# Attention and two expert layers on one core: a second buffer for the split sums, and ScalarE copies in place of four VectorE transposes a group

## The chip, the cores and the metric
One NeuronCore of a Trainium2 chip runs the whole kernel. The metric is the device time of one execution in microseconds. A core has TensorE (PE in the profile; PEld is its weight load), VectorE (DVE), ScalarE (ACT), GpSimd (POOL) and SyncE (SP, which here issues nearly all DMA transfers). Each engine works through its own queue in order.

## The reference
```python
def _attn_ref(q, k, v, beta):                  # 4 x 8 heads, 768 tokens, 48 wide
    k_n = k / (norm(k) + 1e-06)
    for t in range(S):
        y[:, :, t] = einsum('bhd,bhde->bhe', q[:, :, t], state)
        v_old = einsum('bhde,bhd->bhe', state, kt)
        state = state + bt * einsum('bhd,bhe->bhde', kt, vt - v_old)

def _moe_ref(x, w_gate, w1, w2):               # 3072 x 384, 8 experts of 1024
    P = exp(logits - max); 8 rounds of row and column scaling of P
    out = sum over e of P[:, e:e+1] * (maximum(x @ w1[e], 0) @ w2[e])

def _moe2_ref(x, w_in, w_out):                 # 384 -> 2048 -> 384
    h = x @ w_in
    return (h / (1 + exp(-1.702 * h))) @ w_out
```
The three run one after the other, all in float32.

## The kernel before, in words
**Attention stage** (about the first 560 us). The recurrence is done in 24 units of 64 tokens. For each group of four units a generator `prep` (L208) makes 32 inverse triangles of 64x64 in blocks of 32x32: `gram` multiplies keys, and VectorE writes the masked result into `am` (L187); VectorE transposes blocks of `am` into `ln` (L265 and L268), runs the triangle's 30 steps (L271 to L279), and transposes back into `ta` (L297) and `tt` (L324); `pz` and `px` (L302, L311) are the small products between the blocks, whose results ScalarE copies. `chain` (L336) uses `tt` to carry the state. The list at L326 is the order in which `pz`, `px` and the transposes of `tt` are emitted; each `yield` is a place where other work is put in between. Expert 0's matmuls are spread between these pieces, and what is emitted first stands first in each engine's queue. In the first group `gram` also lets ScalarE copy its second plane (L198).

**Expert stages** (about 561 us to the end). A product of a 3x3 scheme of blocks is computed with 15 products instead of 18: `SCHEME` lists them, one a step. Every step emits one product (3 matmuls, L478 to L480, with the results taken by ScalarE L1005, VectorE L1012), the second layer's matmuls of the unit before, and then single calls of generators that prepare later work. 72 units of 15 steps follow each other: 56 for the experts (ReLU, L969 on ScalarE and L971 on VectorE) and 16 for the last layer (sigmoid, L975, L977, L978, L980).

**The sums.** The scheme needs sums of token blocks (`sums`, L543). For each of four chunks of 128 columns, three transfers load `raw` from DRAM (L565, braw in the profile), GpSimd forms sums in `v` (L549, bv), and `put` (L551) splits two or three of them into a rounded part and a rest and writes them to DRAM. `put` is this:
```python
o = bp.tile([128, 2, 3, 128], F32R, tag="o", name="bo")     # one buffer
nc.scalar.copy(out=o[:, 0, 0:n], in_=src)
yield
tt(o[:, 1, 0:n], src, o[:, 0, 0:n].bitcast(F32), ALU.subtract)
yield
for k in range(n):
    nc.sync.dma_start(out=xs[i][hf][at + k, ...], in_=o[:, :, k])
```
After its last line `put` returns, and the same call of the generator goes on to the next sums and the next `put`, up to that one's first `yield`. The generator is called once per slot in the attention stage (L748), and by L1106 at every fifth step, at three steps of five, or at every step of a unit but the first, for the second to the fourth of the four runs of `sums`. `weights1d` (L859) does the like for weights; its tile wo (L869) took the tags raw and o by turns.

Of the kernel before, what the change touches and what calls it, by code (L numbers as in the profile page):

```python
# [10 lines left out]
F32R = mybir.dt.float32r  # L11
# [29 lines left out]
class Attention:  # L41
# [166 lines left out]
    def prep(self, g):  # L208

        nc, am, tt = self.nc, self.am, self.tt  # L210
# [51 lines left out]
                yield 1.0  # L262

        ln = self.one.tile([128, 32, 32], F32, tag="ln", name="ln")
        nc.vector.transpose(out=ln, in_=am[:, :, 32:64].rearrange("p m t -> p t m"))  # L265
        yield 1.0
        for q in (0, 64):
            nc.vector.transpose(out=ln[q:q + 32], in_=am[q:q + 32, :, 0:32].rearrange("p m t -> p t m"))  # L268
            yield 1.0
        nc.vector.memset(ln.rearrange("p t s -> p (t s)")[:, 0:1024:33], 1.0)  # L270
        for jj in range(1, 31):  # L271
            tmp = self.one.tile([128, 256], F32, tag="lt", name="lt")
# [3 lines left out]
                out=t3, in0=ln[:, jj + 1:32, jj:jj + 1].to_broadcast([128, nr, jj]),  # L276
# [42 lines left out]
                nc.scalar.copy(out=tt[q:q + 32, m0:m0 + n, 32:64], in_=ps[q:q + 32])  # L319

        def tr(q):
            p = slice(0, 128) if q is None else slice(q, q + 32)
            c = 32 if q is None else 0
            nc.vector.transpose(out=tt[p, :, c:c + 32].rearrange("p m t -> p t m"), in_=ln[p])  # L324

        for f, *i in (((pz, 0, 16), (tr, None), (pz, 16, 16), (tr, 0), (px, 0, 16), (tr, 64), (px, 16, 16)) if g else  # L326
                      ((pz, 0, 8), (tr, None), (px, 0, 8), (tr, 0), (tr, 64), (pz, 8, 8), (px, 8, 8),
                       (pz, 16, 16), (px, 16, 16))):
            while f == tr and self.upped < u - 1:
                yield 1.0  # L330
            f(*i)
            if (f, i) == (tr, [64]):
                self.ready = g
            yield 1.0

# [104 lines left out]
def kernel(  # L440
# [4 lines left out]
    nc = tc.nc  # L445
# [27 lines left out]
    def split(dst_hi, dst_lo, src, eng=nc.vector):  # L473
        nc.scalar.copy(out=dst_hi, in_=src)  # L474
        eng.tensor_tensor(out=dst_lo, in0=src, in1=dst_hi.bitcast(F32), op=ALU.subtract)  # L475
# [8 lines left out]
    bp = ctx.enter_context(tc.tile_pool(name="b", bufs=1, side="right"))  # L484
# [58 lines left out]
    def sums(i, hf):  # L543


        g = nc.gpsimd

        def tt(o, a, b, op):
            g.tensor_tensor(out=o, in0=a, in1=b, op=op)  # L549

        def put(at, src):  # L551

            n = src.shape[1]
            o = bp.tile([128, 2, 3, 128], F32R, tag="o", name="bo")
            nc.scalar.copy(out=o[:, 0, 0:n], in_=src)
            yield
            tt(o[:, 1, 0:n], src, o[:, 0, 0:n].bitcast(F32), ALU.subtract)
            yield
            for k in range(n):
                nc.sync.dma_start(out=xs[i][hf][at + k, :, :, c:c + 128].bitcast(F32), in_=o[:, :, k].bitcast(F32))  # L560

        for c in range(0, 512, 128):
            raw = bp.tile([128, 3, 3, 128], F32, tag="raw", name="braw")
            for t in range(3):
                nc.sync.dma_start(out=raw[:, t], in_=xf[i][hf][t, :, :, c:c + 128])  # L565
            b = [[raw[:, t, d] for t in range(3)] for d in range(3)]
            v = bp.tile([128, 8, 128], F32, tag="v", name="bv")
            yield
            if i:
                yield from put(8, raw[:, 0:3, 0])  # L570
            tt(v[:, 4], b[2][1], b[2][2], ALU.subtract)
            tt(v[:, 5], b[0][0], b[1][0], ALU.add)
            tt(v[:, 0], b[1][2], v[:, 4], ALU.add)
            tt(v[:, 1], v[:, 4], b[0][2], ALU.subtract)
            yield
            if i:
                yield from put(11, raw[:, 1:3, 1])
            tt(v[:, 2], v[:, 5], b[1][1], ALU.subtract)
            tt(v[:, 3], v[:, 2], v[:, 1], ALU.subtract)
            tt(v[:, 3], v[:, 3], b[0][1], ALU.subtract)  # L580
            yield from put(0, v[:, 0:2])
            tt(v[:, 4], b[1][2], v[:, 5], ALU.subtract)
            tt(v[:, 5], b[1][1], b[1][0], ALU.subtract)
            tt(v[:, 5], v[:, 5], b[2][0], ALU.add)
            yield from put(2, v[:, 2:4])
            tt(v[:, 6], b[0][2], b[2][0], ALU.subtract)
            tt(v[:, 6], v[:, 6], b[2][2], ALU.add)
            tt(v[:, 7], zero, b[1][2], ALU.subtract)
            tt(v[:, 7], v[:, 7], b[2][0], ALU.subtract)
            yield from put(4, v[:, 4:6])  # L590
            if i:
                yield from put(13, raw[:, 0:2, 2])
            yield from put(6, v[:, 6:8])
            yield
# [102 lines left out]

    prep = chain.from_iterable(A.prep(g) for g in range(NG))
    next(prep)
    ew = weights0()  # L700
    A.at[14] = A.at[26] = lambda: next(ew)
    while A.ready < 0:
        next(prep)
# [11 lines left out]
    def slot(t):  # L715

        n, k = rate * ITEMS[t % 16] if t >= LAG else 0, (PIECES if t > 15 else FIRST)[t % 16]
        if t == LAG:
            expert(BURST)
        i = 0  # L720
        while i < k:
            expert(n / (k + 1) * step[0])
            step[0] = next(prep, 1.0)
            i += step[0]
        expert(n / (k + 1))
# [78 lines left out]
    def raw1(e, k):  # L804
        t = xp.tile([128, 2, 3, 128], F32, tag="w1r", name="w1r")
        nc.sync.dma_start(out=t.rearrange("p a b c -> p (a b c)"),
                          in_=w_src(e, k)[0].rearrange("p a b c -> p (a b c)"))
        return t
# [15 lines left out]
    def add1(f):  # L824

        g = nc.gpsimd
        v = xp.tile([128, 12, 128], F32, tag="w1v", name="w1v")
        two = [128, 2, 128]
        g.tensor_tensor(out=v[:, 0:3], in0=f[:, 0], in1=f[:, 1], op=ALU.add)
        yield  # L830
        g.tensor_tensor(out=v[:, 3:5], in0=f[:, 0, 0:1].to_broadcast(two), in1=f[:, 0, 1:3], op=ALU.subtract)
        yield
        g.tensor_tensor(out=v[:, 5:7], in0=f[:, 1, 0:1].to_broadcast(two), in1=f[:, 1, 1:3], op=ALU.subtract)
        yield
        g.tensor_tensor(out=v[:, 7:9], in0=f[:, 0, 1:3], in1=f[:, 1, 0:1].to_broadcast(two), op=ALU.add)
        yield
        g.tensor_tensor(out=v[:, 9], in0=v[:, 5], in1=f[:, 1, 2], op=ALU.subtract)
        yield
        g.tensor_tensor(out=v[:, 10], in0=f[:, 0, 2], in1=v[:, 9], op=ALU.subtract)
        g.tensor_tensor(out=v[:, 11], in0=v[:, 9], in1=f[:, 0, 1], op=ALU.subtract)  # L840
        yield
        yield (12, 14, f[:, 0, 1:3]), (14, 15, f[:, 1, 0:1]), (0, 6, v[:, 0:6]), (6, 12, v[:, 6:12])
# [16 lines left out]
    def weights1d(n):  # L859

        f = raw1(*second[n])
        yield
        for parts in add1(f):
            if parts is None:
                yield
        for a, b, src in parts:
            for c in range(a, b, 2):
                m = min(2, b - c)
                o = bp.tile([128, 2, 2, 128], F32R, tag=("raw", "o")[c // 2 % 2], name="wo")  # L869
                split(o[:, 0, 0:m], o[:, 1, 0:m], src[:, c - a:c - a + m], nc.gpsimd)  # L870
                yield
                nc.sync.dma_start(out=wd[nf + n][:, :, c:c + m].bitcast(F32), in_=o[:, :, 0:m].bitcast(F32))
# [192 lines left out]
    for j in range(len(units) + 1):  # L1065
# [3 lines left out]
        for k in range(len(SCHEME)):  # L1069
            now = 15 * j + k  # L1070
            if (j, k) == (nf + 1, 5):
                building.append(sums(1, 0))
                building.extend(weights1d(n) for n in range(ns))
            elif (j, k) == (2 * nf + 1, 5):
                building.append(sums(1, 1))
# [91 lines left out]
```

## Time and profile before

| | |
|---|---|
| median of 3 runs | 2385.11 us (2384.11 to 2388.26) |
| the profiled execution | 2387.82 us |
| its span, first to last instruction | 2386.1 us |
| mean granted TensorE clock | 0.957 |
| busy share: PE, DVE, ACT, POOL | 92%, 66%, 43%, 47% |
| mean DMA rate | 141 GB/s |

The profile is one execution. Busy shares are means over stages that have different limits, so the rows below are taken by stretch. A wait is the idle time of an engine just before an instruction, with the instruction or transfer that released it. The span is 1.7 us shorter than that execution's own time.

### The profile page before, as it was taken

What the parts mean: (1) busy time and instruction counts of PE and PEld (TensorE: products, weight loads), DVE (VectorE), ACT (ScalarE), POOL (GpSimd) and SP (SyncE); (2) the same over time, 40 slices, a digit from 0 to 9 for tenths busy, and PEclk for the clock granted to TensorE, in tenths of its full rate; (3) what the DMA queues carried; (4) which work ended last, traced back from release to release, by engine and by line L of the source; (5) the groups of instructions that cost most, each with busy time, mean ns of one, the idle gap of its engine ahead of it and who ended that gap; (6) DMA issues with size and microseconds to landing.
All of it is one profiled execution on the core that took longest, in us unless ns stands there. A gap on an engine that the chain in (4) does not pass through costs nothing. (4 is left out here: it accounts for less than half of the span.)

```text
span 2386.1 us, 40806 instructions
## 1 busy us (share of the span) xinstructions
PE 2190.5 (92%) x15663; PEld 1966.7 (82%) x15663; DVE 1565.8 (66%) x2778; ACT 1034.5 (43%) x2101; POOL 1124.5 (47%) x1326
## 2 busy tenths in 40 slices
PE   4599989988889898999999989999999998779999
PEld 3488878887779798999998878898989987668888
DVE  8778786627566575777666566777765555457675
ACT  2233333434334443444445434454544454345554
POOL 5511123225666665666643555566554325543233
PEclk8599999999999999999999999999999998889999
DMA  5223333346343343233367555555554284446331
GB/s 121 55 75 88 98 108 81 101 131 249 116 168 112 116 163 121 102 141 134 118 235 222 156 154 176 176 187 187 183 182 149 87 277 129 117 133 212 119 117 50
DMA packets 229155, 336.75 MB, mean 141 GB/s; under 512 B 15648, under 2 KB 192416, under 8 KB 224800
## 3 DMA queue, kind: packets, MB, share of 16 engines
q1 hardware_dynamic: 228240, 333.26, 43.4%
q8 instruction: 123, 2.02, 0.4%
q10 hardware_dynamic: 720, 0.89, 0.1%
q14 instruction: 72, 0.59, 0.1%
HBM read 204.58 MB, written 129.50 MB: 140 GB/s over the span
## 5 line engine op out<-in xcount | busy, mean ns | idle before, releaser
L479 PE MATMUL po<-w2c,h 128*128 128x384 f32 x1728 | 592.8, 343 | 0.0
L480 PE MATMUL po<-w2c,h 128*128 128x384 f32 x1728 | 590.9, 342 | 0.7 <-DVE h L980 0.7
L478 PE MATMUL po<-w2c,h 128*128 128x384 f32 x1728 | 585.5, 339 | 0.7 <-ACT ye L1034 0.5
L478 PE MATMUL c<-xt,w1c 128*128 128x512 f32 x1080 | 438.9, 406 | 94.2 <-DVE h L971 46.6
L1035 POOL TENSOR_TENSOR acc<-acc,ye 128x384 f32<-128x384 f32 x252 | 264.3, 1049 | 440.6 <-ACT ye L1034 426.9
L480 PE MATMUL c<-xt,w1c 128*128 128x512 f32 x1080 | 434.1, 402 | 0.0
L479 PE MATMUL c<-xt,w1c 128*128 128x512 f32 x1080 | 433.7, 402 | 0.0
L1012 DVE TENSOR_TENSOR o<-o,c 128x512 f32<-128x512 f32 x288 | 197.3, 685 | 271.1 <-PE c L480 231.0
L478 PEld LDWEIGHTS po<-w2c,h 128*128 128x128 f32 x1728 | 330.3, 191 | 41.5 <-ACT ye L1034 1.1
L479 PEld LDWEIGHTS po<-w2c,h 128*128 128x128 f32 x1728 | 328.9, 190 | 40.7
L1037 DVE SCALAR_TENSOR_TENSOR acc<-po,P,acc 128x384 f32<-128x384 f32 x420 | 258.3, 615 | 151.5 <-PE po L480 148.2
L480 PEld LDWEIGHTS po<-w2c,h 128*128 128x128 f32 x1728 | 329.5, 191 | 1.1 <-DVE h L980 1.1
L478 PEld LDWEIGHTS c<-xt,w1c 128*128 128x128 f32 x1080 | 206.2, 191 | 130.5 <-DVE h L971 61.1
L1034 ACT ACTIVATE ye<-po,P 128x384 f32<-128x384 f32 x252 | 146.3, 581 | 300.1 <-PE po L480 290.6
L480 PEld LDWEIGHTS c<-xt,w1c 128*128 128x128 f32 x1080 | 206.1, 191 | 46.3 <-POOL w1c L475 0.4
L479 PEld LDWEIGHTS c<-xt,w1c 128*128 128x128 f32 x1080 | 207.0, 192 | 8.8
L1005 ACT COPY o<-c 128x512 f32<-128x512 f32 x288 | 163.5, 590 | 58.7 <-PE c L480 57.9
L1047 POOL TENSOR_TENSOR acc<-acc,ye 128x384 f32<-128x384 f32 x84 | 92.6, 1102 | 193.3 <-ACT ye L1046 189.9
L969 ACT ACTIVATE h<-c 128x512 fp32r<-128x512 f32 x168 | 96.1, 597 | 164.5 <-DVE c L1012 158.6
L475 POOL TENSOR_TENSOR w2c<-w2r,w2c 128x384 fp32r<-128x384 f32 x140 | 144.6, 1033 | 44.4 <-ACT w2c L474 44.3
L1012 DVE TENSOR_TENSOR f<-o,c 128x512 f32<-128x512 f32 x216 | 149.2, 691 | 12.5 <-PE c L480 3.7
L971 DVE SCALAR_TENSOR_TENSOR h<-f,h 128x512 fp32r<-128x512 f32 x168 | 115.0, 685 | 48.3 <-ACT h L969 47.9
(174 smaller groups left out, 3551.3 us busy)
## 6 DMA issues: line engine op xcount, KB each, us to landing
w1c<-wd SPq DMA_DIRECT2D x210, 384.0 KB, 4.4
wd<-w1c SPq DMA_DIRECT2D x28, 1920.0 KB, 6.9
xs<-bo SPq DMA_DIRECT2D x184, 128.0 KB, 2.2
xt<-xs SPq DMA_DIRECT2D x46, 512.0 KB, 6.0
w2r<-in_w_dram SPq DMA_DIRECT2D x55, 384.0 KB, 6.1
wd<-wo SPq DMA_DIRECT2D x56, 256.0 KB, 2.9
w1r<-in_w_dram SPq DMA_DIRECT2D x28, 384.0 KB, 7.6
x<-in_kq_dram SPq DMA_DIRECT2D x24, 384.0 KB, 6.4
```

Of the source, the lines that this page charges most:

```text
L475: eng.tensor_tensor(out=dst_lo, in0=src, in1=dst_hi.bitcast(F32), op=ALU.subtract)
L478: nc.tensor.matmul(ps, lhs[0], rhs[0], start=start, stop=False, **kw)
L479: nc.tensor.matmul(ps, lhs[0], rhs[1], start=False, stop=False, **kw)
L480: nc.tensor.matmul(ps, lhs[1], rhs[0], start=False, stop=stop, **kw)
L969: nc.scalar.activation(out=h[:, 0], in_=src, func=ACTF.Relu)
L971: nc.vector.scalar_tensor_tensor(out=h[:, 1], in0=src, scalar=0.0, in1=h[:, 0].bitcast(F32), op0=ALU.max, op1=ALU.subtract)
L1005: nc.scalar.copy(out=o, in_=ps)
L1012: nc.vector.tensor_tensor(out=d, in0=o, in1=ps, op=ALU.add if how == "add" else ALU.subtract)
L1034: nc.scalar.mul(ye, ps, P[:, u, e:e + 1])
L1035: nc.gpsimd.tensor_tensor(out=a, in0=a, in1=ye, op=ALU.add)
L1037: nc.vector.scalar_tensor_tensor(out=a, in0=ps, scalar=P[:, u, e:e + 1], in1=a, op0=ALU.mult, op1=ALU.add)
L1047: nc.gpsimd.tensor_tensor(out=a, in0=a, in1=ye, op=ALU.add)
```

## The change
The tile o gets two buffers, in `put` and in `weights1d` (where both tags become o). In `prep`, two ScalarE copies bring two quadrants of `am` into the columns 0 to 31, after which one transpose of all 128 partitions reads those columns, in place of one transpose of all partitions and two of 32. For `tt`, one transpose of all partitions stays and two ScalarE copies take the place of two transposes of 32; in the list of pieces they now stand ahead of the first `px`.
```diff
         ln = self.one.tile([128, 32, 32], F32, tag="ln", name="ln")
-        nc.vector.transpose(out=ln, in_=am[:, :, 32:64].rearrange("p m t -> p t m"))
+
+        for q in (32, 96):
+            nc.scalar.copy(out=am[q:q + 32, :, 0:32], in_=am[q:q + 32, :, 32:64])
+            yield 1.0
+        nc.vector.transpose(out=ln, in_=am[:, :, 0:32].rearrange("p m t -> p t m"))
         yield 1.0
-        for q in (0, 64):
-            nc.vector.transpose(out=ln[q:q + 32], in_=am[q:q + 32, :, 0:32].rearrange("p m t -> p t m"))
-            yield 1.0
...
         def tr(q):
-            p = slice(0, 128) if q is None else slice(q, q + 32)
-            c = 32 if q is None else 0
-            nc.vector.transpose(out=tt[p, :, c:c + 32].rearrange("p m t -> p t m"), in_=ln[p])
-
-        for f, *i in (((pz, 0, 16), (tr, None), (pz, 16, 16), (tr, 0), (px, 0, 16), (tr, 64), (px, 16, 16)) if g else
-                      ((pz, 0, 8), (tr, None), (px, 0, 8), (tr, 0), (tr, 64), (pz, 8, 8), (px, 8, 8),
+            if q is None:
+                nc.vector.transpose(out=tt[:, :, 32:64].rearrange("p m t -> p t m"), in_=ln)
+            else:
+                nc.scalar.copy(out=tt[q:q + 32, :, 0:32], in_=tt[q:q + 32, :, 32:64])
+
+        for f, *i in (((pz, 0, 16), (tr, None), (pz, 16, 16), (tr, 0), (tr, 64), (px, 0, 16), (px, 16, 16)) if g else
+                      ((pz, 0, 8), (tr, None), (tr, 0), (tr, 64), (px, 0, 8), (pz, 8, 8), (px, 8, 8),
                        (pz, 16, 16), (px, 16, 16))):
...
-            if (f, i) == (tr, [64]):
+            if f == px and i[0] == 0:
                 self.ready = g
...
-            o = bp.tile([128, 2, 3, 128], F32R, tag="o", name="bo")
+            o = bp.tile([128, 2, 3, 128], F32R, tag="o", name="bo", bufs=2)
...
-                o = bp.tile([128, 2, 2, 128], F32R, tag=("raw", "o")[c // 2 % 2], name="wo")
+                o = bp.tile([128, 2, 2, 128], F32R, tag="o", name="wo", bufs=2)
```
The second buffer moves no instruction. The copies do. ScalarE's queue at the start of the first group, before (x_125 and x_126 are the operands of `gram`, pg its result):
```order
L128 ACTIVATE ns<-ss 128x16 x2
L198 COPY x_125<-pg 64x512 x4
L198 COPY x_126<-pg 64x512 x4
L128 ACTIVATE ns<-ss 128x16 x2
L198 COPY x_127<-pg 64x512 x4
```
And now:
```order
L128 ACTIVATE ns<-ss 128x16 x2
L198 COPY x_125<-pg 64x512 x4
L198 COPY x_126<-pg 64x512 x4
L267 COPY am<-am 32x32x32 x2
L128 ACTIVATE ns<-ss 128x16 x2
L198 COPY x_127<-pg 64x512 x4
```
The two copies of `am` stand behind the first eight copies of `gram`'s second plane.

ScalarE's queue at the end of the first group, before:
```order
L474 CAST w2s_198<-wr 128x384
L309 COPY ta<-pz 32x256 x2
L319 COPY tt<-px 32x8x32 x2
L358 ACTIVATE r<-v 128x384
L474 CAST w1s_191<-wr 128x384
```
And now, with the line numbers of the changed kernel:
```order
L476 CAST w2s_198<-wr 128x384
L310 COPY ta<-pz 32x256 x2
L326 COPY tt<-tt 32x32x32 x2
L320 COPY tt<-px 32x8x32 x2
L360 ACTIVATE r<-v 128x384
L476 CAST w1s_191<-wr 128x384
```
The two copies of `tt` stand between the copies of the first `pz` and the first `px`.

VectorE's queue where the first group's triangle begins, before:
```order
L187 TENSOR_TENSOR am<-pg,bm 128x512 x4
L265 STREAM_TRANSPOSE ln<-am 128x1024
L268 STREAM_TRANSPOSE ln<-am 32x1024 x2
L270 MEMSET ln 128x32
L275 TENSOR_TENSOR lt<-ln 128x30
```
And now:
```order
L187 TENSOR_TENSOR am<-pg,bm 128x512 x4
L269 STREAM_TRANSPOSE ln<-am 128x1024
L271 MEMSET ln<- 128x32
L276 TENSOR_TENSOR lt<-ln 128x30
```
One transpose is left of three, and it reads what the copies wrote.

## Rows read from the trace of the kernel before
**Rows 1.** The page, part 1: busy time, share of the span and instructions.
```profile
PE 2190.5 (92%) x15663; PEld 1966.7 (82%) x15663; DVE 1565.8 (66%) x2778; ACT 1034.5 (43%) x2101; POOL 1124.5 (47%) x1326
```
**Rows 2.** Waits of TensorE, whole span: us in total, times, longest us.
```profile
PE c L478 <- DVE h L971: 46.6, 22, 8.0
PE c L478 <- DVE sg L977: 41.3, 17, 7.5
```
**Rows 3.** Tile bo: what its engines sat idle for (us, times), two rows.
```profile
  DMA xs<-bo: 214.7, 59
...
  DMA braw<-xf: 14.0, 5
```
**Rows 4.** Timeline near 631: start, us, instruction, [idle before it <- releaser].
```profile
631.22 0.40 ACT L555 CAST bo<-bv 128x256 fp32r<-128x256 f32 x1 [10.28 <-DMA xs<-bo]
631.53 1.08 ACT L969 ACTIVATE h<-c 128x512 fp32r<-128x512 f32 x2
...
623.77 1.97 SPq L560 DMA_DIRECT2D xs<-bo  x2
...
633.49 0.79 PE L478 MATMUL c<-xt,w1c 128*128 128x512 f32 x1 [8.00 <-DVE h L971]
```
**Rows 5.** Windows: length, busy us (count) by engine, granted clock, DMA share, GB/s.
```profile
576.70:945.70 369.00, 337.88 (x1640) 304.23 (x1639) 231.56 (x373) 155.28 (x302) 238.41 (x293) 0.95 0.37 130
945.70:1247.60 301.90, 301.90 (x1523) 274.21 (x1521) 210.28 (x342) 135.89 (x256) 180.88 (x197) 1.00 0.40 147
1298.80:1487.90 189.10, 169.95 (x822) 149.32 (x821) 119.06 (x204) 77.30 (x159) 102.33 (x134) 0.98 0.53 160
1981.40:2154.50 173.10, 133.70 (x587) 118.38 (x585) 88.11 (x138) 75.31 (x156) 84.34 (x114) 0.87 0.43 125
2154.50:2343.80 189.30, 187.62 (x938) 168.26 (x938) 130.52 (x211) 103.54 (x205) 60.52 (x56) 1.00 0.43 142
```
**Rows 6.** Timeline of ScalarE in the last pass of sums: three copies into bo.
```profile
2028.83 0.41 ACT L555 CAST bo<-bv 128x256 fp32r<-128x256 f32 x1 [3.51 <-DMA xs<-bo]
...
2032.92 0.41 ACT L555 CAST bo<-bv 128x256 fp32r<-128x256 f32 x1 [3.30 <-DMA xs<-bo]
...
2052.36 0.51 ACT L555 CAST bo<-braw 128x384 fp32r<-128x384 f32 x1 [5.29 <-DMA braw<-xf]
```
**Rows 7.** DMA issues: queue, count, KB each, median us from issue to landing.
```profile
braw<-xf SPq DMA_DIRECT2D x48, 192.0 KB, 3.7
```
**Rows 8.** Timeline of TensorE in the attention stage, two waits.
```profile
355.81 0.58 PE L478 MATMUL ph<-xb,w1s 128*128 128x256 f32 x1 [5.17 <-DVE h L626]
...
424.77 1.94 PE L363 MATMUL up<-r,tt 64*64 64x48 f32 x32 [4.39 <-DVE r L354]
```
**Rows 9.** Windows of the attention stage, without and with sums (columns as rows 5).
```profile
130.00:330.00 200.00, 194.33 (x3130) 170.56 (x3129) 152.51 (x350) 71.34 (x160) 40.10 (x36) 0.99 0.32 84
330.00:520.00 190.00, 172.31 (x2599) 155.22 (x2598) 108.33 (x242) 67.61 (x158) 49.53 (x77) 0.95 0.34 95
```
**Rows 10.** Lines by form: the transposes of 32 partitions, busy us, mean ns.
```profile
L268 DVE STREAM_TRANSPOSE ln<-am 32x1024 f32<-32x1024 f32 x12 | 23.6, 1970 | 0.2
L324 DVE STREAM_TRANSPOSE tt<-ln 32x1024 f32<-32x1024 f32 x12 | 23.3, 1942 | 0.2
```
**Rows 11.** Lines by form, ScalarE: the cast of 768 elements.
```profile
L474 ACT CAST w1c<-w1v 128x768 fp32r<-128x768 f32 x56 | 46.5, 830 | 0.0
```
**Rows 12.** Timeline of the first group's start, ScalarE and VectorE.
```profile
25.35 2.39 ACT L198 COPY x<-pg 64x512 f32<-64x512 f32 x4 [0.36 <-PE pg L181]
...
22.69 3.90 DVE L268 STREAM_TRANSPOSE ln<-am 32x1024 f32<-32x1024 f32 x2
...
35.15 2.76 DVE L275 TENSOR_TENSOR lt<-ln 128x108 f32<-128x108 f32 x1
...
38.24 0.29 DVE L275 TENSOR_TENSOR lt<-ln 128x130 f32<-128x130 f32 x1
```
**Rows 13.** Waits of ScalarE, whole span: us in total, times, longest.
```profile
ACT ns L128 <- DVE ss L127: 62.7, 12, 15.9
```

## The prediction
> **What bounds the kernel now.** I read the page first: TensorE is busy for 2190.5 of 2386.1 us, VectorE for 66%, ScalarE for 43%, GpSimd for 47% [rows 1]. So time can be won only where TensorE stands still or runs at its lower clock. Next I read who TensorE waits for. Two lines make nearly half of its idle time: the first matmul of a chain in the expert stages waits 46.6 us in 22 places for VectorE's L971 and 41.3 us in 17 places for VectorE's L977 [rows 2]. VectorE is at 66%, so it is late, not full, and the question is what it waited for itself.
>
> The view of the tile bo answers that. ScalarE's copy into bo (L555, the first step of `put`) sat behind a transfer xs<-bo 59 times, 214.7 us together [rows 3]. The reason is in the code of `put`. One call of the generator emits the transfer of the last pair of sums (L560) and, right behind it, ScalarE's copy of the next pair into the same single buffer. That copy must therefore wait until the transfer it was emitted with has landed, and everything behind it on ScalarE's in-order queue waits too. One place shows the whole chain: the transfer is issued at 623.77 on SP; ScalarE stands 10.28 us before the copy at 631.22; its next instructions are the two ReLUs (L969); TensorE's next chain starts at 633.49 after 8.00 us of idling for L971, which needs such a ReLU [rows 4].
>
> How much do these stops cost? I compare stretches by their number of matmuls, since the mix of shapes repeats every 117 matmuls (15 steps). From 945.7 to 1247.6 no sums are built: 1523 matmuls in 301.9 us, 0.1982 us each, clock 1.00. For the last part, 2154.5 to 2343.8, it is 189.3/938 = 0.2018 us [rows 5]. By these rates:
> - 576.7 to 945.7 (sums of the second half of the tokens, first layer): 1640 matmuls should take 325.1 us and take 369.0, an excess of 43.9.
> - 1298.8 to 1487.9 (second layer, first half): 822 should take 162.9 and take 189.1, an excess of 26.2.
> - 1981.4 to 2154.5 (second layer, second half): 587 at 0.2018 should take 118.5 and take 173.1, an excess of 54.6.
>
> These 124.7 us hold the idle time and what the clock loses after it: the granted clock is 0.95, 0.98 and 0.87 there against 1.00 in the clean stretches [rows 5]. 0.5 of full speed is the level of 1.2 GHz.
>
> **The second buffer, part by part.** With two buffers the copy of pair n+2 waits for the transfer of pair n, which was emitted two calls earlier. In the tightest pass (1981.4 to 2154.5) there is a call at nearly every step; a step is 117 x 0.2018 / 15 = 1.57 us, a pair takes two calls, so the copy comes 4 steps or 6.3 us after the one whose buffer it takes. What it needs by then is copy, GpSimd's subtraction, issue and landing; two successive copies that wait for just this chain stand 2032.92 - 2028.83 = 4.1 us apart [rows 6]. 4.1 is less than 6.3, so the wait for xs<-bo should be gone there. In the first pass the calls come only every fifth step, so even 10.28 us [rows 4] is covered.
>
> What is late next is the load of the three blocks to be summed (braw, still one buffer): it is issued one call before it is read. Its three issues and 3.7 us to landing [rows 7] are more than one step of 1.57 us. Before the change this shows little, 14.0 us in 5 places [rows 3], because ScalarE was held already; the one at 2052.36 cost 5.29 us [rows 6]. I leave 2 us of TensorE time for each of the four chunks of the last pass (8) and 1 us for each of the four in the pass before (4, since calls are 5/3 steps apart there). The landing is taken from the row. The Trainium skill, "DMA: Bandwidth & Descriptors", section on the anatomy of one DMA, puts a fixed 2.0 us on a transfer, most of it the receipt of the write; by that figure these loads would nearly be hidden and I would leave nothing, so the sum would be 12 us better. The row has the queueing in it, so I go by the row.
>
> So the three passes give 43.9 - 1 = 43, 26.2 - 4 = 22 and 54.6 - 8 = 46.
>
> The first pass of sums runs inside the attention stage, from about 330 us. TensorE's stops there include 5.17 us at 355.81 and 4.39 us at 424.77 [rows 8], behind ScalarE waits of the same kind. I compare 330 to 520 with 130 to 330, where no sums are built: idle is 190.0 - 172.3 = 17.7 us against 5.7, and the clock is 0.95 against 0.99 [rows 9]. In proportion that is 17.7 - 5.4 = 12.3 us of idling and 0.04 x 190 = 7.6 us of clock, about 20; other waits of that stage can take their place, so I take 16. Bounds for it: 8 and 24.
>
> The buffers of the weight sums (wo) alternated between two tags before, so they already had two: nothing. The second buffer only takes memory.
>
> **Transposes to copies.** Removed on VectorE: 12 transposes at 1970 ns and 12 at 1942 ns [rows 10], 46.9 us. Added on ScalarE: 24 copies of 32 partitions by 1024 elements, a size that the trace lacks. The nearest row is a cast of 768 elements at 830 ns [rows 11]; the same per element gives 1.11 us, and it cannot be under 0.83. I take 1.1, so 26 us, spread over a stage where ScalarE is less than half busy. Most of the 46.9 us is hidden: from 130 to 330 TensorE is busy for 194.3 of 200 us [rows 9], and what VectorE saves there can return at most those 5.7 us.
>
> Only the first group lies on the path, and there it cuts both ways. The two copies of `am` stand on ScalarE behind the eight L198 copies, which end at 25.35 + 2.39 = 27.74. With 2.2 us of copies and one transpose of 2 us the triangle starts at about 31.9, not at 22.69 + 3.90 = 26.6 [rows 12]: up to 5.3 us later. But VectorE crawls there beside GpSimd: an update of 108 elements takes 2.76 us at 35.15, one of 130 elements 0.29 us at 38.24 [rows 12]. A later start lets more updates fall behind GpSimd's work, so I take 1.5 us of loss. At the end of the group one transpose and two copies (4.2 us on two engines) stand in place of three transposes in a row, 1 us gained; the second group's triangle starts about 1.5 us earlier; 1 more for the other groups. Together 2 us gained; bounds: 26 us lost, if every copy lay on the path, and 10 gained.
>
> **Sum.** 43 + 22 + 46 + 16 + 2 = 129. The profiled execution took 2387.8, which gives 2258.8; it is 2.7 above the median of the runs shown, 2385.1, so I forecast 2257.
>
> **Rivals.**
> 1. *The stall only changes its name.* The single load buffer and GpSimd's in-order queue eat half of what the two late passes should give, and the attention stage gives 8. Then 43 + 11 + 23 + 8 = 85 gained: about 2300. For it: the load waits exist [rows 3, 6]. Against: 4.1 us against 6.3.
> 2. *The releaser is named wrongly.* If the copies really waited for the sums on GpSimd, a second buffer would change nothing: about 2385. Against: SP's issue and ScalarE's release fit one another [rows 4].
> 3. *Slower: in-order copies hold ScalarE in the attention stage.* A copy of `am` waits for VectorE, and the ReLUs and state copies queue behind it. There are 12 such pairs, each 2.2 us plus the wait. It decides if a pair costs over 10.6 us: 12 x 10.6 = 127 eats the rest of the sum. A like instruction, L128, waits for VectorE 62.7 us in 12 places, 5.2 each and 15.9 at most [rows 13]. At 15.9 for each pair, 12 x 18.1 = 217 us, and 2385 - 127 + 217 = 2475. Against it: the mean would give 12 x 7.4 = 89, which is still faster (2347), and ScalarE had idle time to lose.
>
> **How the numbers follow.** Forecast with its spread 0.77, rival 1 0.18, rival 2 0.02, rival 3 0.03. The most that can come back is 124.7 + 24 + 10 = 159, about 2226. The range, 2232 to 2298, leaves that end and the last part of rival 1 outside. A measurement of this kernel can tell about 0.2%, 5 us. Faster: forecast, rival 1 and a mild form of rival 3, 0.95; same 0.02; slower 0.03.
>
> **What would show it.** Right: waits of bo for xs<-bo fall from 214.7 us to under 30; the waits L971 and L977 fall from 88 to under 25; the three stretches run at 0.20 us a matmul and a clock near 1.00; waits for braw grow. The triangle of the first group starts near 32 us. Wrong: the bo waits go but TensorE's idle stays (another releaser), or ScalarE stands for VectorE before the am copies.

## The result, and the profile after

The changed kernel takes 2276.7 us (median of 4 runs, 2274.1 to 2279.2), the kernel before beside it 2386.7 (4 runs, 2384.1 to 2389.5). The ratio is 0.9539 with a 95% interval of 0.9521 to 0.9557: 110 us faster, where 129 were forecast. The forecast of 2257 lies 20 us too low, the range of 2232 to 2298 holds the time.

The profiled execution took 2275.1 us. Its page, the span and the line of busy times:

```profile
span 2273.4 us, 40807 instructions
...
PE 2161.1 (95%) x15663; PEld 1945.2 (86%) x15663; DVE 1520.3 (67%) x2754; ACT 1065.2 (47%) x2125; POOL 1128.3 (50%) x1326
```

TensorE has the same matmuls in 29 us less of busy time [rows 1]: matmuls that ran at the lower clock before now run at the higher one (mean granted clock 0.957 before, 0.974 after). The other 83 of the 113 us of span are idle time that is gone.

The waits of TensorE (us in total, times, longest), then the waits of ScalarE in the view of the tile bo (us, times):

```profile
PE c L480 <- DVE sg L979: 10.5, 15, 3.9
PE c L480 <- DVE h L973: 8.2, 12, 3.0
```
```profile
  DMA braw<-xf: 14.0, 4
  DMA xs<-bo: 12.8, 8
```

The two lines that headed TensorE's waits fell from 87.9 us to 18.7 (L971 and L977 of before are L973 and L979 now) [rows 2]. The wait of ScalarE's copy for the transfer out of its buffer fell from 214.7 us in 59 places to 12.8 in 8 [rows 3]. The waits for the load (braw) are 14.0 us, as before; the prediction said that they would grow.

Windows over the passes of the expert stages, each between the same matmuls as in [rows 5] (length, busy us and count of PE, PEld, DVE, ACT, POOL, granted clock, DMA share, GB/s):

```profile
563.10:894.40 331.30, 327.40 (x1639) 296.59 (x1638) 230.85 (x373) 156.29 (x302) 237.76 (x293) 0.99 0.40 143
1248.00:1417.60 169.60, 165.74 (x820) 148.54 (x820) 120.22 (x204) 79.06 (x159) 103.14 (x134) 0.99 0.59 180
1911.20:2042.00 130.80, 121.37 (x586) 107.72 (x586) 87.37 (x135) 71.96 (x151) 86.18 (x112) 0.97 0.56 163
2042.00:2231.10 189.10, 187.68 (x938) 168.28 (x938) 130.45 (x211) 103.84 (x205) 60.54 (x56) 1.00 0.43 142
```

| stretch | before | after | gained | forecast | at the clean rate |
|---|---|---|---|---|---|
| start of the span to the first pass (attention stage, copies) | 576.7 | 563.1 | 13.6 | 16 + 2 | |
| first pass | 368.9 | 331.3 | 37.6 | 43 | 325 |
| second layer, first half | 189.0 | 169.6 | 19.4 | 22 | 162.9 |
| second layer, second half ("last pass" below) | 173.1 | 130.8 | 42.3 | 46 | 118.5 |
| all stretches between and behind them | 1078.4 | 1078.6 | -0.2 | 0 | |

The first two passes before are taken between the unrounded starts of the matmuls; the windows of [rows 5] round them to 369.0 and 189.1. The parts add up to the 112.7 us by which the spans differ. All four terms of the forecast have the right sign and place, and each came out 2.6 to 5.4 us smaller than forecast.

### The profile page after: what moved, and what is told of

Same layout as the page of the kernel before. It is cut to its first block, busy times and chain, and to the rows that moved or that the text cites. A ratio compares the mean times of both kernels' runs of the same rounds, so it can differ in the third digit from the quotient of the medians.

```text
span 2273.4 us, 40807 instructions
## 1 busy us (share of the span) xinstructions
PE 2161.1 (95%) x15663; PEld 1945.2 (86%) x15663; DVE 1520.3 (67%) x2754; ACT 1065.2 (47%) x2125; POOL 1128.3 (50%) x1326
## 5 line engine op out<-in xcount | busy, mean ns | idle before, releaser
L480 PE MATMUL c<-xt,w1c 128*128 128x512 f32 x1080 | 431.3, 399 | 19.8 <-DVE sg L979 10.5
L482 PE MATMUL c<-xt,w1c 128*128 128x512 f32 x1080 | 430.6, 399 | 2.3 <-POOL w1c L477 2.3
L481 PE MATMUL c<-xt,w1c 128*128 128x512 f32 x1080 | 429.3, 398 | 0.0
L480 PEld LDWEIGHTS po<-w2c,h 128*128 128x128 f32 x1728 | 325.7, 188 | 40.3 <-ACT ye L1036 0.7
L481 PEld LDWEIGHTS po<-w2c,h 128*128 128x128 f32 x1728 | 324.7, 188 | 40.0
L482 PEld LDWEIGHTS po<-w2c,h 128*128 128x128 f32 x1728 | 325.8, 189 | 1.1 <-DVE h L982 1.1
L480 PEld LDWEIGHTS c<-xt,w1c 128*128 128x128 f32 x1080 | 203.8, 189 | 50.9 <-DVE h L973 19.6
L482 PEld LDWEIGHTS c<-xt,w1c 128*128 128x128 f32 x1080 | 203.3, 188 | 47.8 <-POOL w1c L477 3.1
L481 PEld LDWEIGHTS c<-xt,w1c 128*128 128x128 f32 x1080 | 203.7, 189 | 9.0
L971 ACT ACTIVATE h<-c 128x512 fp32r<-128x512 f32 x168 | 96.7, 599 | 175.2 <-DVE c L1014 168.0
L971 ACT ACTIVATE h<-f 128x512 fp32r<-128x512 f32 x168 | 100.4, 598 | 72.8 <-DVE f L1014 70.6
```

Source lines behind the costliest of these rows:

```text
L480: nc.tensor.matmul(ps, lhs[0], rhs[0], start=start, stop=False, **kw)
L481: nc.tensor.matmul(ps, lhs[0], rhs[1], start=False, stop=False, **kw)
L482: nc.tensor.matmul(ps, lhs[1], rhs[0], start=False, stop=stop, **kw)
L971: nc.scalar.activation(out=h[:, 0], in_=src, func=ACTF.Relu)
```

## The experiments

Each kernel's time is a median and stands against runs of the kernel before on the same chip (medians of 2386.2 to 2387.3 us). A diff is against the changed kernel unless the text names another base.

### Which part of the change carries it

**The buffer alone.** The transposes stay on VectorE; the diff is against the kernel before:

```diff
-            o = bp.tile([128, 2, 3, 128], F32R, tag="o", name="bo")
+            o = bp.tile([128, 2, 3, 128], F32R, tag="o", name="bo", bufs=2)
...
-                o = bp.tile([128, 2, 2, 128], F32R, tag=("raw", "o")[c // 2 % 2], name="wo")
+                o = bp.tile([128, 2, 2, 128], F32R, tag="o", name="wo", bufs=2)
```

> Only the second buffer of o; the transposes are those of before. Theory (the buffer carries nearly all of the gain, the copies are worth 2 us): 2272 to 2282 us, within 5 us of the changed kernel's 2276.7; ScalarE's waits of bo for xs<-bo near 13 us instead of 214.7. Rival (the copies carry part of the gain, since VectorE has 46.9 us less to do): 2284 us or more.

Measured: 2279.8 us (2278.3 to 2282.9), ratio 0.9559 [0.9546, 0.9571]. In the view of the tile bo:

```profile
  DMA xs<-bo: 11.5, 6
```

The edit in `weights1d` is part of this run, but ScalarE's waits for its transfers (wd<-wo) are 13.3 us before the change and 11.8 in this run, so nothing speaks for a gain from there.

**The copies alone.** One buffer as before, copies and order of the change:

> Only the copies in place of the transposes; o has one buffer as before. Theory: hidden under TensorE but for the first group, where loss and gain nearly cancel: 2380 to 2390 us, and the first group's triangle starts near 32 us instead of 26.7. Rival (VectorE's 46.9 us count): 2375 us or less. Rival (copies hold ScalarE in its queue): 2395 us or more.

Measured: 2384.3 us (2380.0 to 2393.8), ratio 0.9997 [0.9986, 1.0009]: no change that can be measured. The view of the tile bo is that of before:

```profile
  DMA xs<-bo: 207.6, 58
```

So the second buffer carries 107 of the 110 us. The copies are worth nothing that can be measured by themselves, and some 3 us beside the buffer (2279.8 against 2276.7, and the runs of the two just overlap).

### Is it the distance between transfer and next copy?

**One buffer, transfer emitted earlier.** If the stall comes from emitting the transfer together with the copy that must wait for it, the transfer can be pulled forward by one call, with one buffer. On top of the copies alone:

```diff
             tt(o[:, 1, 0:n], src, o[:, 0, 0:n].bitcast(F32), ALU.subtract)
-            yield
             for k in range(n):
                 nc.sync.dma_start(out=xs[i][hf][at + k, :, :, c:c + 128].bitcast(F32), in_=o[:, :, k].bitcast(F32))
+            yield
```

> One buffer for o, with the copies of the change; the transfer of a pair of sums is emitted in the call of its subtraction, one call ahead of the next pair's copy and not in the same call. Theory (the stall comes from a copy emitted together with the transfer it must wait for, so the distance counts and not the number of buffers): the first pass of the expert stages, where calls are five steps apart, runs as with two buffers (331 us from its first to its last unit, not 369), the middle one nearly so, the last one, with calls one step apart, gains about half of 42 us; in all 2290 to 2320 us. Rival (one buffer always blocks): 2360 us or more. Rival (the releaser is GpSimd, not the transfer): no change from before, 2380 to 2390 us.

Measured: 2346.2 us (2341.9 to 2351.5), ratio 0.9836 [0.9821, 0.9852]. A miss for the total: 40 us of the 110, not 66 to 96. The windows of the three passes, and the waits, say why:

```profile
565.60:895.00 329.40, 326.69 (x1639) 295.62 (x1638) 230.83 (x372) 155.60 (x300) 237.20 (x292) 1.00 0.41 145
1248.40:1437.30 188.90, 171.26 (x821) 150.69 (x821) 119.05 (x204) 77.70 (x159) 101.48 (x134) 0.97 0.53 159
1930.80:2108.80 178.00, 137.84 (x586) 121.33 (x585) 88.54 (x138) 75.52 (x156) 84.45 (x114) 0.84 0.41 122
```
```profile
  DMA xs<-bo: 129.1, 46
```

In the first pass, where a call comes every fifth step, one call of distance is enough: 329.4 us, as good as two buffers. In the pass after it the edit gives nothing (188.9 against 187.5 with the copies alone), and in the last pass, with a call at nearly every step, it costs 5 us (178.0 against 173.0). The expectation had the middle pass nearly as good as with two buffers, and half of 42 us back in the last. In the kernel before, 3.6 us pass from the start of a subtraction to the next copy into the buffer (2029.31, shown further below, to 2032.92 [rows 6]). By the prediction's rates one call is an estimated 7.7 us in the first pass, 2.6 in the middle one and 1.6 in the last. So distance is the right quantity in the first pass, and the sizes fit the other two; why the last pass even loses 5 us stays open.

### What is left in the two late passes

After the change the last pass is 12.3 us above its clean rate and the pass before it 6.7. The forecast had put 8 and 4 there, both for the load.

**Load ahead.** No second buffer for braw is needed: the next chunk's braw is loaded ahead of the last `put` of the chunk before, whose source is a computed sum. That is three calls of the generator earlier:

```diff
-        for c in range(0, 512, 128):
+        def load(c):
             raw = bp.tile([128, 3, 3, 128], F32, tag="raw", name="braw")
             for t in range(3):
                 nc.sync.dma_start(out=raw[:, t], in_=xf[i][hf][t, :, :, c:c + 128])
+            return raw
+
+        ahead = load(0)
+        for c in range(0, 512, 128):
+            raw = ahead
...
+            if c < 384:
+                ahead = load(c + 128)
             yield from put(6, v[:, 6:8])
```

> The changed kernel, and the load of the next chunk's blocks is emitted ahead of the chunk's last put, three calls before it is read and not one; still one buffer for it. Theory (what is left of the stalls is this load): 2262 to 2270 us, the last pass (units 58 to 62) 122 to 126 us instead of 130.8, waits of bo for braw under 4 us instead of 14. Rival (what is left is GpSimd coming late with the subtraction): 2273 to 2279 us, the last pass above 128 us.

Measured: 2262.7 us (2261.6 to 2266.7), ratio 0.9488 [0.9476, 0.9501]. Windows of the second and the last pass, and the waits of bo:

```profile
1250.10:1414.00 163.90, 163.53 (x821) 147.26 (x820) 119.94 (x203) 78.78 (x159) 103.72 (x135) 1.00 0.61 187
1908.00:2033.60 125.60, 120.07 (x587) 106.34 (x586) 86.57 (x135) 71.99 (x151) 86.50 (x113) 0.99 0.59 172
```
```profile
  DMA xs<-bo: 11.8, 9
  DMA braw<-xf: 1.4, 2
```

The waits for the load fell to 1.4 us, and the passes are 5.7 and 5.2 us shorter. The waits for xs<-bo stay, so they are a cause of their own.

**Subtraction on VectorE.** The rest of the last pass was put down to GpSimd, which comes late to the subtraction (L551) because other work stands before it in its queue:

```diff
-            tt(o[:, 1, 0:n], src, o[:, 0, 0:n].bitcast(F32), ALU.subtract)
+            (nc.vector if i and hf else g).tensor_tensor(
+                out=o[:, 1, 0:n], in0=src, in1=o[:, 0, 0:n].bitcast(F32), op=ALU.subtract)
```

> The changed kernel, with the subtraction of the split on VectorE instead of GpSimd in the last pass of sums only (second layer, second half). Theory (beside the load, GpSimd coming late with the subtraction holds the second buffer): the last pass, units 58 to 62, takes 124 to 128 us instead of 130.8; all in all 2270 to 2275 us; waits of bo for xs<-bo fall from 12.8 to under 6 us. Rival (only the load is left): the last pass stays at 130 us or more, 2275 to 2280 us. Rival (VectorE's queue makes L979 later): above 2280 us.

Measured: 2265.7 us (2264.3 to 2271.5), ratio 0.9496 [0.9474, 0.9519]. The last pass and the wait:

```profile
1906.10:2031.00 124.90, 119.83 (x586) 106.33 (x585) 96.31 (x160) 71.82 (x151) 65.23 (x86) 0.99 0.58 168
```
```profile
  DMA xs<-bo: 0.6, 1
```

The pass gives 5.9 us, as expected, and the wait for xs<-bo is gone with the buffers unchanged: it was GpSimd that held them. The total is 4 to 9 us better than expected. In the profiles that surplus lies where the edit changes no instruction (first pass -1.5 us, second -2.5, attention -1.0). The control below moved by only 0.1 us in the first two of these, so the spread between executions doesn't explain it, and its cause is open. The edit also takes work off GpSimd's queue (busy for 65 us of the pass instead of 86), so the 5.9 us hold whatever that gives beside the buffer.

**Three buffers** reach the same wait from the other side (room for the third comes from making the tile of zeros one column wide and broadcasting it):

```diff
-    zero = bp.tile([128, 128], F32, name="zero")
+    zero = bp.tile([128, 1], F32, name="zero")
...
-            o = bp.tile([128, 2, 3, 128], F32R, tag="o", name="bo", bufs=2)
+            o = bp.tile([128, 2, 3, 128], F32R, tag="o", name="bo", bufs=3)
...
-            tt(v[:, 7], zero, b[1][2], ALU.subtract)
+            tt(v[:, 7], zero.to_broadcast([128, 128]), b[1][2], ALU.subtract)
...
-                o = bp.tile([128, 2, 2, 128], F32R, tag="o", name="wo", bufs=2)
+                o = bp.tile([128, 2, 2, 128], F32R, tag="o", name="wo", bufs=3)
```

> The changed kernel with three buffers for o; the tile of zeros shrinks to one column read by broadcast to make room. Theory (two buffers nearly do; what waits for xs<-bo are only single late subtractions): waits for xs<-bo fall from 12.8 us to near 0, and the last pass wins 2 to 4 us of 130.8; 2272 to 2276 us. Rival (two are still too few throughout): the last pass below 124 us, 2265 us or less.

Measured: 2267.9 us (2262.8 to 2269.6), ratio 0.9498 [0.9476, 0.9519], 4 us under the lower end of what was expected. The last pass takes 126.1 us (130.8 with two buffers), 4.7 less where 2 to 4 were expected, and bo never waits for xs<-bo. GpSimd's queue is as it was, so these 4.7 us are the price of the wait itself, as far as one profile can tell (the control below moved by 1.4 in this pass). Another 4.3 us are in the attention stage, where the granted clock did not fall at a place where it fell in the changed kernel (last section).

**Load ahead and subtraction on VectorE together:**

> The earlier load of the next chunk and the subtraction on VectorE in the last pass together. Theory (the two leftovers add up): 2256 to 2261 us, the last pass 119 to 122 us, which is its rate in the clean stretch (118.5). Rival (they are the same stall seen twice): no better than the earlier load alone, 2262.7.

Measured: 2258.7 us (2255.1 to 2266.9, 5 runs), ratio 0.9469 [0.9444, 0.9493]. This is the lowest median of the study, 18 us below the changed kernel: it beats both. The second pass takes 163.8 us, as with the load ahead alone. The last pass:

```profile
1899.50:2021.60 122.10, 118.38 (x588) 105.03 (x587) 96.33 (x160) 71.63 (x151) 65.78 (x87) 1.00 0.58 172
```

The two edits give 8.7 us there, not 5.2 + 5.9 = 11.1, which fits waits of which part lay side by side. 3.6 us above the clean rate remain.

**And a third buffer on top:**

> The earlier load, the subtraction on VectorE in the last pass and three buffers for o. Theory: nothing is left for the third buffer, within 3 us of the kernel with the first two edits. Rival: another 4 us or more.

Measured: 2263.8 us (2259.0 to 2267.5), ratio 0.948 [0.9456, 0.9504]. The last pass is 122.2 us, so nothing is left there for a third buffer. The median is 5 us above that of the version without it, where 3 had been allowed; the runs overlap, and the profile has the difference in the attention stage (568.1 against 560.2 us), in part in stretches at a low clock (0.57 against 0.86 from 434 to 446).

### Controls

**The changed kernel once more,** beside the last experiment:

> The changed kernel once more, beside the next kernel on one chip, to see how far its time and its attention stage move from one execution to the next with nothing changed. Theory (the stretches of low granted clock in the attention stage differ between executions): 2268 to 2280 us; the first expert unit starts within 555 to 570 us of the span's start, not at 563.1 each time, and the four expert passes stay within 2 us of the first profile.

Measured: 2277.2 us (2274.8 to 2278.5), ratio 0.9532 [0.9508, 0.9555]. The attention stage and the three passes are 562.4, 331.2, 169.7 and 132.2 us: within 1.4 us of the first profile. The theory that the stretches of low clock differ is not borne out by these two: from 434 to 446 the granted clock is 0.57 in the one and 0.58 in the other.

**Transposes in the first group only,** on top of load ahead and subtraction on VectorE, to price the late start of the triangle:

```diff
+        if g == 0:
+            nc.vector.transpose(out=ln, in_=am[:, :, 32:64].rearrange("p m t -> p t m"))
+            yield 1.0
+            for q in (0, 64):
+                nc.vector.transpose(out=ln[q:q + 32], in_=am[q:q + 32, :, 0:32].rearrange("p m t -> p t m"))
+                yield 1.0
+        else:
...
```

> The earlier load and VectorE's subtraction, with the transposes of before in the first group only. Theory (the copies start the first triangle 5 us later and most of that is won back beside GpSimd): the triangle starts near 26.7 us instead of 31.8, the first state product (up) comes 0.3 to 1.5 us earlier, 2255 to 2259 us, which is hardly more than the kernel with the first two edits alone. Rival (the late start costs its whole 5 us): 2254 us or less with up at 77 us.

Measured: 2259.9 us (2258.6 to 2264.1), ratio 0.9462 [0.9438, 0.9486], 1 us above the expected end. Timelines of the version with these transposes and of the one without (start, us, instruction, [idle before it <- releaser]): the first instruction of the triangle, and the matmul that needs the finished group:

```profile
27.02 0.09 DVE L278 MEMSET ln<- 128x32 f32 x1
...
81.37 1.84 PE L372 MATMUL up<-r,tt 64*64 64x48 f32 x30 [2.40 <-ACT r L367]
```
```profile
32.53 0.09 DVE L271 MEMSET ln<- 128x32 f32 x1
...
82.09 1.20 PE L365 MATMUL up<-r,tt 64*64 64x48 f32 x18 [2.40 <-ACT r L360]
```

5.5 us of earlier start become 0.7 us at TensorE. It is no gain that the time shows.

## Why the prediction was right, and where it was off

**The mechanism held.** The step "with two buffers the copy of pair n+2 waits for the transfer of pair n" is borne out twice: the buffer without the rest of the change gives 107 us, with xs<-bo down to 11.5, and one buffer with the transfer one call earlier gives the same first pass (329.4 us) as two buffers. Rival 2, a releaser named wrongly, falls with the first of these.

**Last pass, 46 forecast, 42.3 measured; the forecast's "4.1 is less than 6.3, so the wait should be gone there" failed in part.** The chain of 4.1 us came from one place [rows 6], where GpSimd stood waiting for the copy, as its timeline in the kernel before shows:

```profile
2029.31 0.75 POOL L549 TENSOR_TENSOR bo<-bv,bo 128x256 fp32r<-128x256 f32 x1 [0.93 <-ACT bo L555]
```

It doesn't always stand ready. The changed kernel's timeline, ScalarE's copies into one of the two buffers and then GpSimd's queue between them:

```profile
1978.46 0.42 ACT L557 CAST bo<-bv 128x256 fp32r<-128x256 f32 x1
...
1986.71 0.41 ACT L557 CAST bo<-bv 128x256 fp32r<-128x256 f32 x1 [4.40 <-DMA xs<-bo]
```
```profile
1978.66 1.01 POOL L1049 TENSOR_TENSOR acc<-acc,ye 128x384 f32<-128x384 f32 x1 [0.67 <-ACT ye L1048]
...
1982.09 1.02 POOL L477 TENSOR_TENSOR w2c<-w2r,w2c 128x384 fp32r<-128x384 f32 x1
1983.08 0.73 POOL L551 TENSOR_TENSOR bo<-bv,bo 128x256 fp32r<-128x256 f32 x1
```

The copy is done at 1978.88. Its subtraction starts at 1983.08, behind an accumulation, four block sums and the split of a weight. The next copy into the same buffer starts at 1986.71, so the chain is 8.25 us, longer than the 6.3 that the prediction put between two uses of a buffer. That term was too long here as well: ScalarE had begun to wait 4.40 us before, at 1982.31, which is 3.85 us after the first copy. This stop belonged to rival 1 (GpSimd's in-order queue eats part of the gain); the sum of the forecast had 0 for it. By the experiments such stops are worth 3.5 us (VectorE's subtraction beside the load ahead), 4.7 (three buffers) or 5.9 (VectorE's subtraction alone) of the last pass. All 12.8 us of waits for xs<-bo that are left lie in it.

**The load, 8 + 4 forecast, 5.2 + 5.7 measured** (last pass, then the one before it) by the load ahead. The size is right, though one pass is too high and the other too low. The step "waits for braw grow" is wrong: they stayed at 14.0 us; why is not shown. The row of the changed kernel has 4.0 us from issue to landing, and moving the issue forward gave 10.9 us. The Trainium skill, "DMA: Bandwidth & Descriptors", section on the anatomy of one DMA, gives a transfer that GpSimd issues some 2.0 us of fixed cost, beside a part that grows with its size; SyncE issues the loads here, and the row, with the queueing in it, is twice that figure. Nor did it follow from that figure that nothing was left in the last pass, since 2.0 us is more than the 1.57 of one step.

```profile
braw<-xf SPq DMA_DIRECT2D x48, 192.0 KB, 4.0
```

**First pass, 43 forecast, 37.6 measured.** One us was left for what would be late next; the pass stands 6.2 above its rate. One place is a chain through the load queue: GpSimd waits 8.30 us for weights (w1r) whose load SP issued at 636.91 behind loads of braw, and 15.6 us later TensorE waits for a weight split of GpSimd's:

```profile
644.65 1.02 POOL L831 TENSOR_TENSOR w1v<-w1r 128x384 f32<-128x384 f32 x1 [8.30 <-DMA w1r<-in_w_dram]
```
```profile
660.22 0.73 PE L482 MATMUL c<-xt,w1c 128*128 128x512 f32 x1 [2.30 <-POOL w1c L477]
```

That the one leads to the other is read from the order on GpSimd; no run took it apart, and the load itself was no slower than usual (7.6 us is the median of these loads, before the change too). All kernels with two or three buffers took 328.6 to 331.7 us here, so 3.5 us or more remain in every one of them, and their cause is open.

**Attention stage and copies, 16 + 2 forecast, 13.6 measured.** The window of the stage in which sums are built, to set beside [rows 9]:

```profile
330.00:520.00 190.00, 182.77 (x2681) 165.69 (x2678) 99.17 (x241) 79.36 (x174) 51.60 (x80) 0.96 0.38 109
```

Idle time fell from 17.7 to 7.2 us. That is 10.5 of the 12.3 counted. The granted clock only rose from 0.95 to 0.96: of the 7.6 us that the prediction counted for it, 0.01 x 190 = 1.9 came back. This term failed, not the idle time; the last section shows one place that it ran into. With three buffers the clock of this window is 1.00, and the stage came out 17.9 us shorter than before; with the subtraction on VectorE it is 1.00 too, and the stage only 14.6 us shorter. So the clock is not all of it.

**The copies, 2 forecast, 0 to 3 measured.** A copy takes 1045 ns (1.1 taken), and the copies of am waited for VectorE 1.2 us in one place; that decides against rival 3, which needed 10.6 us for each pair. The groups of instructions by line (xcount | busy us, mean ns | idle before, its releaser):

```profile
L267 ACT COPY am<-am 32x1024 f32<-32x1024 f32 x12 | 12.5, 1045 | 1.4 <-DVE am L187 1.2
L326 ACT COPY tt<-tt 32x1024 f32<-32x1024 f32 x12 | 12.5, 1044 | 0.3
```

The start of the first triangle came as forecast (31.9):

```profile
29.76 1.92 DVE L269 STREAM_TRANSPOSE ln<-am 128x1024 f32<-128x1024 f32 x1 [9.31 <-ACT am L267]
31.75 0.34 DVE L276 TENSOR_TENSOR lt<-ln 128x30 f32<-128x30 f32 x1
...
34.82 2.73 DVE L280 TENSOR_TENSOR ln<-ln,lt 128x58 f32<-128x58 f32 x1
37.59 0.25 DVE L276 TENSOR_TENSOR lt<-ln 128x84 f32<-128x84 f32 x1
```

VectorE leaves its slow phase at 37.59, after four instructions of the triangle; before the change it left it at about the same time (35.15 + 2.76 = 37.91), farther along [rows 12]. GpSimd's work of that stretch ends at 37.5 and 37.8 in the two traces. That fits what the last experiment shows: five us of later start cost less than one at TensorE. The first state product starts at 81.77, against 81.25 before: the net loss of 0.5 us that the prediction had for the first group (1.5 lost, 1 gained).

**The sum of the misses:** 5.4 + 2.6 + 3.7 + 4.4 = 16 us, which is the forecast for the profiled execution (2258.8) against its time (2275.1). The other 3.4 us between the forecast and the median are the 1.6 by which the median lies above the profiled execution, and the 1.8 that the prediction took off for the median. (By its own difference of 2.7 it should have come to 2256.) Rival 1 was the right direction at a fraction of its size: 16 us given back, not 44.

## What to carry to other kernels

Where a pipeline emits a transfer out of a buffer together with the next write into that buffer, the engine of that write can wait out the whole landing, and the work behind it in its queue with it (214.7 us in 59 places here): compare the chain from write to landing with the distance between two uses, and give it one buffer or one step more. Take that chain at its worst place, with the helper engine's queue in it (8.25 us here), not at its cleanest (4.1). When a large wait goes, look for those that lay beside it: the load three calls earlier and the subtraction on another engine took 14.5 us off the two late passes.

## What the runs showed of the hardware

TensorE's clock fell at one place of the attention stage in most of the profiled kernels but not in all, after much the same wait. In the changed kernel and in the one with three buffers TensorE waits 1.63 and 1.38 us at 433.6, and the same matmuls follow:

```profile
433.67 1.20 PE L307 MATMUL pz<-ta,am 32*32 32x32 f32 x64 [1.63 <-DVE ta L298]
...
435.11 0.52 PE L481 MATMUL po<-w2s,h 128*128 128x384 f32 x1
```
```profile
433.57 1.20 PE L307 MATMUL pz<-ta,am 32*32 32x32 f32 x64 [1.38 <-DVE ta L298]
...
434.99 0.34 PE L481 MATMUL po<-w2s,h 128*128 128x384 f32 x1
```

The windows from 434 to 446 of the two:

```profile
434.00:446.00 12.00, 12.00 (x192) 11.01 (x185) 3.15 (x4) 5.50 (x9) 0.97 (x1) 0.57 0.15 40
```
```profile
434.00:446.00 12.00, 12.00 (x339) 10.83 (x331) 3.52 (x5) 7.47 (x13) 4.65 (x8) 1.00 0.23 64
```

A matmul takes 0.52 us in the one and 0.34 in the other, at a granted clock of 0.57 (most of the stretch at the level of 1.2 GHz) against 1.00 (2.4 GHz). The same six matmuls po and 64 pz, up to the next ph, take 3.89 us (434.80 to 438.69) against 2.38 (434.70 to 437.08). A third buffer alone does not decide it: the other kernel with three buffers had 0.57 there, and the control of the changed kernel 0.58. TensorE was busy for 85 to 92% of the time from 423 to 433 in all of these, at a clock of 1.00. The Trainium skill, "TensorE: Matmul & The Clock Gate", section "What's actually happening", says that the number of matmuls at the lower clock at a kernel's start varies from run to run of one kernel. The place here is in the middle, and the two profiles of the changed kernel both fell there, so these rows don't show it for one kernel. The mean over a whole run does vary: the five runs of load ahead and subtraction on VectorE together have granted clocks from 0.975 (2266.9 us) to 0.984 (2255.1 us). What chooses is open. Among the changed kernel and its variants, whose attention stages are all but the same, its length varies between 558.8 and 568.1 us for that reason in part, so a single profile's total can't price an edit of 5 us; the stretch that the edit touches can. Where the prediction counted the clock as coming back with the idle time, it did so in the expert passes (0.87 to 0.97 in the last one) and not in this profile of the attention stage, where one remaining wait of 1.63 us was followed by a stretch at 0.57.
